# Batch 2's q transposes moved from TensorE to the DMA engines, with the k and q loads of later batches put off

## Chip, cores, metric

One core of a Trainium2 chip. The metric is the device time of the whole program in microseconds (us).

## The reference

Linear attention with an ELU feature map, then two dense layers with a SiLU between, cut to what matters (8 batches, 8 heads, 576 rows, head size 64; the model width is 512, the hidden width 2048):

```python
phi = lambda x: np.where(x > 0, x, np.exp(x) - 1.0) + 1.0
q_p, k_p = phi(q), phi(k)
kv  = einsum('bhsd,bhse->bhde', k_p, v)          # "k product"
num = einsum('bhsd,bhde->bhse', q_p, kv)         # "numerator"
den = einsum('bhsd,bhd->bhs', q_p, k_p.sum(2)) + 1e-6
x   = (num / den) reshaped to 4608 x 512         # "normalisation"
h   = x @ w_in                                   # first phase of a batch
out = (h * sigmoid(beta * h)) @ w_out            # second phase of a batch
```

## The kernel before

TensorE works batch by batch: a first phase (`h_phase`), then a second (`y_phase`). The next batch's attention is threaded between these matmuls by a plan: step number to a list of small jobs. Batch 1's second phase is a special one. It has four output tiles open at once and computes batch 2's attention:

```python
    y_phase_wide(1, {
        1: [F(phi, 2, 1), F(phi, 2, 0)],
        6: [F(kv_mm, 2), F(kv_evac, 2)],
        7: [F(q_trans, 2, 0, 1, wide=True, dve=True)],
        8: [F(q_trans, 2, 2, 3, wide=True, dve=True)],
        9: [F(q_trans, 2, 4, wide=True, dve=True), F(num_mm, 2, 0), F(num_norm, 2, 0)],
        10: [F(num_mm, 2, 1), F(num_norm, 2, 1)],
        11: [F(num_mm, 2, 2), F(num_norm, 2, 2), F(x_trans, 2, 0, wide=True)],
        ...
    def q_trans(b, *ts, wide=False, dve=False):
        ...                                    # 4 transposes on TensorE for each row tile t
        copy(st[b, "qT"][...], tp[...], dve)   # PSUM to SBUF
    def q_trans_dma(b):                        # batches 3 and later do it so already
        nc.sync.dma_start_transpose(out=st[b, "qT"]..., in_=st[b, "p"][:, 0]...)
    def x_trans(b, t, wide=False, dve=False):
        ...                                    # 4 transposes on TensorE into a PSUM bank
        copy(x_dst(b, t), tp[:, :, :n], dve)   # emptied by ScalarE unless dve=True
    def y_phase_wide(b, plan):
        yp = [mm_bank([P, DM]) for _ in range(4)]
        for ff in range(12):
            for t in range(4):
                y_mm(b, yp[t], t, ff)
            run(plan, ff)
        for t in range(4):
            for ff in range(12, FC):
                y_mm(b, yp[t], t, ff)
            y_out(b, t, yp[t], on_act=True)    # output copy on ScalarE
            run(plan, 12 + t)
```

Numerators and wide transposes share two PSUM slots ("att" banks). Ahead of this phase ScalarE makes the exponentials of batch 2, and during it those of batch 3, then loads the SiLU table again (`silu_table`). Loads of k, q and v go through one queue that GpSimd feeds.

## Time and profile before

The time is 296.88 us (median of 3 runs, 296.63 to 297.01); the profiled span is 295.1 us.

| quantity | before |
|---|---|
| TensorE busy | 285.1 us, 97% |
| ScalarE busy | 175.5 us, 59% |
| VectorE busy | 125.2 us, 42% |
| start of batch 1's second phase | 67.15 |
| from there to batch 2's first phase | 18.91 us |
| from there to batch 3's k product | 30.60 us |

The last two rows are my rulers. Both are differences of start times in TensorE's timeline, so the start-up, which shifts by up to 0.9 us from run to run, drops out of them. (Timeline lines are merged: a row stands for a run of like instructions.) In a timeline line the columns are start, duration, engine, source line, operation, tiles and shapes, count, and in brackets the idle time just before with what ended it. Durations of matmuls overlap, so costs are taken from differences of starts.

### The profile page before, as it was taken

The page shows a single profiled execution, that of the slowest core. Times are in us where ns is not written, and L with a number is a line of the kernel's source. Part 1 is how long each engine was busy: PE and PEld are TensorE (multiplying, and loading weights), DVE is VectorE, ACT ScalarE, POOL GpSimd, SP SyncE. Part 2 cuts the span into 40 slices and gives each one's busy share as a digit, 9 for nine tenths or more (in the row PEclk, how much of TensorE's full clock was granted, in tenths as well). Part 3 has the DMA queues.
Part 4 walks back from the last instruction along what each step waited for, and adds up shares of the span by engine and source line. Part 5 has one row for each costly group of instructions (what it writes and reads, how often), then busy time and mean ns, then how long its engine had stood idle before and what let it go on. Part 6 is the DMA issues. An engine that isn't in the chain of part 4 may idle for free.

```text
span 295.1 us, 4791 instructions
## 1 busy us (share of the span) xinstructions
PE 285.1 (97%) x1911; PEld 144.9 (49%) x1932; DVE 125.2 (42%) x264; ACT 175.5 (59%) x234; POOL 52.2 (18%) x72
## 2 busy tenths in 40 slices
PE   8979999999999999999999999999999999999994
PEld 2557445644565544445444544454445444444443
DVE  5675388504772174616461646164715400110012
ACT  2798786889988770778077808790770077018500
POOL 8925475544006000320020000000000000000000
PEclk9999999999999999999999999999999999999998
DMA  7999999999939943698357445024502400120032
GB/s 109 189 205 344 255 273 192 257 193 190 164 142 150 180 93 98 130 177 151 98 128 79 73 116 126 2 72 115 127 0 73 117 36 0 38 94 13 2 71 71
DMA packets 69719, 36.43 MB, mean 123 GB/s; under 512 B 38321, under 2 KB 64193, under 8 KB 69697
## 3 DMA queue, kind: packets, MB, share of 16 engines
q0 software_dynamic: 38912, 20.45, 47.7%
q1 hardware_dynamic: 30624, 15.55, 21.0%
q8 instruction: 15, 0.25, 0.4%
q10 hardware_dynamic: 160, 0.13, 0.2%
q14 instruction: 8, 0.06, 0.0%
HBM read 36.71 MB, written 9.44 MB: 156 GB/s over the span
## 4 chain that ended last, share of the span: by engine, by line
PE 71%; DMA 17%; ACT 4%; POOL 4%; issue 3%; DVE 0%; POOLq 0%; ACTq 0%
PE mm L453 33%; PE mm L505 32%; DMA xqk<-in_q_dram 9%; DMA vraw<-in_v_dram 4%; DMA w_in<-in_moe_w_in_dram 4%; PE att L399 2%; ACT e L229 2%; POOL xqk L131 1%; PE att L344 1%; PE mm L537 1%; ACT L229 1%; POOL vraw L131 1%; ACT g L445 1%; POOL w_in L159 1%; ACT L445 0%
## 5 line engine op out<-in xcount | busy, mean ns | idle before, releaser
L445 ACT ACTIVATE g<-mm,beta_c 128x512 bf16<-128x512 f32 (+2 forms) x156 | 97.3, 633 | 88.1 <-PE mm L453 87.8
L505 PE MATMUL mm<-w_out,g 128*128 128x512 bf16 x541 | 127.2, 379 | 1.2 <-issue 0.3
L453 PE MATMUL mm<-xT,w_in 128*128 128x512 bf16 (+2 forms) x560 | 107.8, 349 | 1.2 <-DMA w_in<-in_moe_w_in_dram 0.8
L453 PEld LDWEIGHTS <-w_in 128*128 128x128 bf16 x656 | 62.0, 98 | 62.0 <-DMA w_in<-in_moe_w_in_dram 1.0
L505 PEld LDWEIGHTS <-g 128*128 128x128 bf16 x560 | 52.7, 98 | 57.3
L515 DVE COPY y_sb<-mm 128x512 f32<-128x512 f32 x27 | 18.7, 692 | 70.4 <-PE mm L505 67.4
L229 ACT ACTIVATE e<-xqk 128x2560 bf16<-128x2560 bf16 x14 | 31.9, 2329 | 0.1
L415 DVE TENSOR_TENSOR xs<-att,rden 128x512 bf16<-128x512 f32 (+1 forms) x40 | 27.6, 689 | 1.6 <-DVE rden L414 0.2
L242 DVE TENSOR_TENSOR qk_p<-r,e 128x2560 bf16<-128x2560 bf16 x14 | 20.9, 1490 | 13.1 <-ACT e L229 12.4
L355 DVE CAST kv_bd<-att 64x130 bf16<-64x130 f32 x28 | 8.2, 292 | 34.5 <-PE att L344 34.1
L72 POOL DMA_DIRECT2D vraw<-in_v_dram x7 | 6.8, 972 | 77.4 <-DVE vaug L370 70.9
L413 DVE TENSOR_SCALAR den<-att 128x8 f32<-128x8 f32 (+1 forms) x40 | 6.5, 162 | 27.0 <-PE att L399 26.8
L399 PEld LDWEIGHTS <-q_pT 128*128 128x128 bf16 (+1 forms) x160 | 11.7, 100 | 10.7 <-DVE xs L415 2.1
L399 PE MATMUL att<-kv_bd,q_pT 128*128 128x130 bf16 (+1 forms) x160 | 15.8, 221 | 1.1 <-DVE kv_bd L370 0.7
L453 PE MATMUL mm<-xT_tail,w_in 128*128 128x512 bf16 x63 | 13.9, 379 | 0.1
L237 DVE TENSOR_SCALAR r<-xqk 128x2560 bf16<-128x2560 bf16 x14 | 11.9, 858 | 3.9 <-DMA xqk<-in_q_dram 2.3
L572 PE MATMUL mm<-g 128*128 128x512 bf16 x34 | 10.4, 468 | 1.2 <-DVE g L143 1.2
L72 POOL DMA_DIRECT2D xqk<-in_k_dram x7 | 8.0, 1150 | 10.2 <-ACT e L229 3.6
L229 ACT ACT_TABLE_LOAD x7 | 9.0, 1283 | 0.1
L414 DVE RECIPROCAL rden<-den 128x8 f32<-128x8 f32 (+1 forms) x40 | 8.1, 201 | 1.4
L72 POOL DMA_DIRECT2D xqk<-in_q_dram x7 | 6.5, 924 | 6.9 <-ACT g L445 2.1
L256 ACT ACTIVATE e<-xqk 128x1280 bf16<-128x1280 bf16 (+1 forms) x4 | 4.4, 1154 | 5.1 <-DMA xqk<-in_k_dram 4.6
(72 smaller groups left out, 142.5 us busy)
## 6 DMA issues: line engine op xcount, KB each, us to landing
out_dram<-y_sb SPq DMA_DIRECT2D x28, 256.0 KB, 2.3
xqk<-in_k_dram POOLq DMA_DIRECT2D x7, 512.0 KB, 10.7
xqk<-in_q_dram POOLq DMA_DIRECT2D x7, 512.0 KB, 11.8
vraw<-in_v_dram POOLq DMA_DIRECT2D x7, 512.0 KB, 11.5
w_in<-in_moe_w_in_dram POOLq DMA_DIRECT2D x4, 512.0 KB, 11.3
g<-in_moe_w_out_dram POOLq DMA_DIRECT2D x4, 512.0 KB, 10.9
out_dram<-y_sb SPq DMA_DIRECT2D x14, 128.0 KB, 5.1
xqk<-in_moe_w_out_dram POOLq DMA_DIRECT2D x2, 512.0 KB, 14.3
```

Source lines behind the costliest of these rows:

```text
L72: eng.dma_start(out=dst[:, :, 0:NJ, :].rearrange("p h j d -> p h (j d)"), in_=src[b, :, 0:MAIN, :].rearrange("h (p j) d -> p h (j d)", j=NJ),)
L229: nc.scalar.activation(st[b, "e", a][:, h0:h1], xqk[b % NX][:, a, h0:h1], ACTF.Exp)
L237: nc.vector.tensor_scalar(st[b, "r", a][:, h0:h1], xqk[b % NX][:, a, h0:h1], 0.0, 1.0, ALU.max, ALU.add)
L242: nc.vector.tensor_tensor(st[b, "p"][:, a].rearrange("p j (h d) -> p h j d", h=H)[:, h0:h1], st[b, "r", a][:, h0:h1], st[b, "e", a][:, h0: ...
L355: nc.vector.tensor_copy(kv_bd[b % 2][i][gs, :, g, :], st[b, "kvp"][gs, 2 * i : 2 * i + 2, :])
L399: nc.tensor.matmul(nps[:n, p // 2, c0 : c0 + 2 * (D + 1)], st[b, "qT"][:, t, p, :n], kv_bd[b % 2][p // 2][:, p % 2], start=True, stop=True ...
L415: nc.vector.tensor_mul(xs[:n], nv[:, :, :, 0:D], rden[:n, :, :, None].to_broadcast([n, 2, 4, D]))
L445: nc.scalar.activation(g_sb[b % 2][:, ff, c0:c1], hp[:, c0:c1], ACTF.Silu, scale=beta_c[:, ff : ff + 1],)
L453: nc.tensor.matmul(hp[:, c0:c1], w_in_sb[ff // 4][:, kc, (ff % 4) * P : (ff % 4 + 1) * P], x[:, t0:t1, kc, :] if b < B else x[:, kc, c0:c1 ...
L505: nc.tensor.matmul(yp, g_sb[b % 2][:, ff, t * P : (t + 1) * P], w_out_sb[ff // 4][:, ff % 4, :], start=(ff == 0), stop=(ff == FC - 1),)
L515: nc.vector.tensor_copy(y_sb, yp)
L572: nc.tensor.matmul(st["warm"], g_sb[0][:, FC - 1, 0:P], g_sb[0][:, FC - 1, :], start=True, stop=True, skip_group_check=True,)
```

## The change

The intent: take 20 transposes off the engine that bounds the kernel. phi(q) is made ahead of phi(k) so that the DMA transpose can start early; batch 5's k and q, which would share the DMA engines with it, are loaded behind batch 5's v, which is held back by a buffer. What is left moves later.

```diff
     def load_next(b):
         if b < B:
+            if b >= 5:
+                load_v(b)
             load_k(b)
             load_q(b)
-            load_v(b)
+            if b < 5:
+                load_v(b)
 ...
-            8: [F(begin, 2), F(relu, 2, 1)],
-            10: [F(relu, 2, 0)],
+            8: [F(begin, 2), F(relu, 2, 0)],
+            10: [F(relu, 2, 1)],
 ...
-    h_last(1, xT[1], [F(exp_, 2, 1), F(exp_, 2, 0)])
+    h_last(1, xT[1], [F(exp_, 2, 0), F(exp_, 2, 1)])
 ...
-        1: [F(phi, 2, 1), F(phi, 2, 0)],
+        1: [F(phi, 2, 0), F(q_trans_dma, 2), F(phi, 2, 1)],
         6: [F(kv_mm, 2), F(kv_evac, 2)],
-        7, 8, 9: q_trans of row tiles 0 to 4;  9 to 13: numerators 0 to 4;  11 to 14: x_trans 0 to 3
+        11: [F(num_mm, 2, 0), F(num_norm, 2, 0)],
+        12: [F(num_mm, 2, 1), F(num_norm, 2, 1), F(x_trans, 2, 0, wide=True)],
+        13: [F(num_mm, 2, 2), F(num_norm, 2, 2), F(x_trans, 2, 1, wide=True)],
+        14: [F(num_mm, 2, 3), F(num_norm, 2, 3)],
 ...                                      # batch 2's first phase
-            plan = {1: [F(x_trans, 2, 4)]}
+            plan = {
+                0: [F(x_trans, 2, 2), F(num_mm, 2, 4), F(num_norm, 2, 4)],
+                1: [F(x_trans, 2, 3)],
+                3: [F(x_trans, 2, 4)],
+            }
```

(The line "7, 8, 9" sums up eight removed lines.)

## The prediction

> **What bounds the kernel now.** I read the busy line first, then the chain of waits, then the timelines of TensorE (PE), ScalarE (ACT) and VectorE (DVE) through the one stretch that the change edits, then the DMA view. The page:
>
> ```profile
> PE 285.1 (97%) x1911; PEld 144.9 (49%) x1932; DVE 125.2 (42%) x264; ACT 175.5 (59%) x234; POOL 52.2 (18%) x72
> PEclk9999999999999999999999999999999999999998
> ```
>
> PE is busy 97% of 295.1 us at the full clock, so a lasting gain must take work or stalls out of PE's stream. The edited stretch is batch 1's second matmul phase: 64 matmuls of 512 columns, with batch 2's attention threaded between. Its first matmul starts at 67.15 and batch 2's first phase at 86.06, 18.91 us later. PE in its second half:
>
> ```profile
> 73.28 0.82 PE L344 MATMUL att<-vaug,qk_p 128*64 128x65 bf16 x40
> 74.27 0.81 PE L505 MATMUL mm<-w_out,g 128*128 128x512 bf16 x3 [0.16 <-issue]
> 74.91 0.61 PE L380 MATMUL att<-identity,qk_p 128*128 128x128 bf16 x8
> 75.36 1.03 PE L505 MATMUL mm<-w_out,g 128*128 128x512 bf16 x4
> ...
> 77.63 0.29 PE L380 MATMUL att<-identity,qk_p 64*128 64x64 bf16 x4
> 77.85 0.41 PE L399 MATMUL att<-kv_bd,q_pT 128*128 128x130 bf16 x4
> 78.09 1.02 PE L505 MATMUL mm<-w_out,g 128*128 128x512 bf16 x4
> ...
> 80.57 0.40 PE L433 MATMUL att<-identity,xs 128*128 128x128 bf16 x4
> 81.02 0.81 PE L505 MATMUL mm<-w_out,g 128*128 128x512 bf16 x3
> 82.12 0.39 PE L399 MATMUL att<-kv_bd,q_pT 128*128 128x130 bf16 x4 [0.29 <-ACT xT L372]
> ```
>
> L380 is the q transposes that go, L399 the numerator, L433 the x transposes, L505 the main matmuls. Durations overlap, so costs come from differences of starts: four main matmuls take 0.86 (75.36 to the next L380 at 76.22), four numerator matmuls 0.24, four x transposes 0.22. Gaps with no work: 80.28 to 80.57 (0.29), 81.66 to 82.12 (0.46; one matmul record of the four seems missing), and 0.10 before the last numerator: 0.85 us lost. ScalarE explains the largest:
>
> ```profile
> 75.51 4.56 ACT L229 ACTIVATE e<-xqk 128x2560 bf16<-128x2560 bf16 x2
> 80.09 1.28 ACT L578 ACT_TABLE_LOAD   x1
> 81.38 0.20 ACT L578 ACTIVATE small<-small 128x1 f32<-128x1 f32 x1
> 81.49 0.58 ACT L372 ACTIVATE xT<-att 128x512 bf16<-128x512 bf16 x1
> 81.97 0.59 ACT L513 ACTIVATE y_sb<-mm 128x512 f32<-128x512 f32 x1
> ```
>
> Batch 3's exponentials and the return to the SiLU table hold ACT until 81.49; only then can it empty the first x transpose's PSUM bank, for which PE stands at 82.12. The chain of waits follows ACT here, not PE.
>
> **What the Trainium skill says.** "VectorE: DVE Perf Modes", section "The three transpose paths", gives 390 ns on TensorE and 1309 ns by DMA for one 128x128 block. Alone, PE is the faster; in a stream the trace has 8 transposes in 0.45 us (74.91 to 75.36), 56 ns each, so the price on PE is far less than 390. "DMA: Bandwidth & Descriptors", section "Queues, rings and completion order", says each DMA engine takes turns between the queues with work, packet by packet; so a transpose beside loads is slowed, not locked out. The trace agrees: 128 KB stores of batch 0, beside saturated loads, landed in 5.3 us (median), those at the end alone in 2.3. "ScalarE: Activation LUTs", section "What ACT_TABLE_LOAD costs", says about 1283 ns for a switch; the page here has 7 of mean 1283.
>
> **The change part by part.**
>
> 1. *Removed from PE:* 5 groups of 4 transposes. Two groups of 8 cost 0.45 each, the tail's 4 cost 0.22 (77.63 to 77.85): 1.12 us of PE's own stream. This is the whole direct gain.
>
> 2. *Removed from DVE:* three copies of q_pT, 0.69 + 0.69 + 0.29 = 1.67 us. DVE is 42% busy; nothing on the path.
>
> 3. *Swapped:* q's exp and phi come before k's. phi(q) takes 68.26 to 69.75, phi(k) 70.49 to 71.98. K's product starts on PE at 73.28, so the swap leaves 1.3 us; no cost.
>
> 4. *Added:* one 640 KB DMA transpose, issued at about 69.8. Those of later batches:
>
> ```profile
> q_pT<-qk_p SPq DMA_TRANSPOSE x5, 4.9
> ```
>
> Alone it would land at 74.7. The loads in flight are the question:
>
> ```profile
> 69.80:75.50 5.70, 5.54 (x69) 3.06 (x69) 2.66 (x5) 5.65 (x7) 1.85 (x3) 1.00 1.59 191
> 75.50:80.00 4.50, 4.50 (x37) 2.46 (x35) 3.24 (x9) 4.49 (x2) 0.00 (x0) 1.00 1.54 183
> 80.00:82.00 2.00, 1.65 (x12) 0.84 (x12) 1.54 (x4) 1.97 (x5) 0.00 (x0) 1.00 0.32 26
> ```
>
> The last two columns are DMA share and GB/s: loads saturate the engines until 80. Batch 4's v (issued 63.34, landing 11.5 us later) fills the time to about 75.5; batch 5's k and q, issued at 68.5 and 71.2, fill 75.5 to 80. The change takes the second part away. So the transpose shares only with v: stretched by 5.3/2.3 for some 6 to 8 us, then alone. At 1/2.3 speed for 6.5 us it does 2.8 of its 4.9; the rest brings it to about 78.4. My estimate is a landing at 77 to 79.
>
> 5. *Moved:* batch 5's k and q are issued behind v(5), which waits for batch 3's vaug copy on DVE. That copy ends at 90.4 now, and some 2 us later once the last normalisation stands before it (part 6); batch 3's k product needs it only near 97. The loads would land near 108 and are first read by the exponentials in batch 3's second phase, near 131. Batches 6 and 7 move back by one v in the same way (landing near 137 and 167, read near 161 and 191). No cost.
>
> 6. *Later plan:* the first numerator now follows step 11, the last numerator and two x transposes move into batch 2's first phase. The work is the same (0.24 + 0.22 + 0.22 = 0.68 us moved).
>
> **Walking PE through the new order.** K's product ends at 74.05 in both. Five steps of 0.86 bring PE to 78.36. Numerator 0 to 78.60; main matmuls to 79.45; numerator 1 to 79.69. X transpose 0 needs DVE's normalisation: in the trace that ends 1.57 us after its numerator starts (77.85 to 79.42), so 79.93, and PE goes on at 79.99 (0.30 lost) to 80.22. Main matmuls to 81.08, numerator 2 to 81.31. X transpose 1 takes the PSUM bank of x transpose 0 (the built program puts both in bank 6), which ACT must empty. ACT is free at 81.49 as before, but its order is now first the output copy, which takes 0.48 of it, then the xT copy of 0.58: done at 82.55, PE goes on at 82.61. That is 1.30 us lost. From there: transpose 0.22, main matmuls 0.86, numerator 3 0.24, main matmuls 0.86: 84.79. Add the 0.68 moved on: 85.47 stands against 86.06. Gain: 0.59 us. Check by sums: 1.12 removed, stalls of 0.30 + 1.30 in place of 0.85, rest rounding.
>
> In batch 2's first phase the same walk, bank by bank, gives no new stall: ACT runs some 0.1 us ahead of each bank that PE wants. After that all is PE-bound (gaps of about 0.2 us a batch at most), so the shift is carried to the end: 296.88 - 0.59 = 296.3.
>
> **The rivals.**
>
> *The full gain.* If ACT's wait were not there, PE would keep 1.12 us and lose only the 0.30: 0.85 + 1.12 - 0.30 = 1.67, giving 295.2. Against it: exp, table load and copies on ACT are untouched by the change, and end at 81.49 whatever PE does. The removed work frees PE to arrive earlier at the same wait. That is why I take half of 1.12.
>
> *The transpose lands late.* It is needed at 78.36 by numerator 0. But PE has the 1.30 us wait ahead of it anyway: a landing up to about 79.5 only shifts idle time from one place to the other. Beyond that each us costs one. If the 2.3 stretch held to the end it would land at 69.8 + 11.3 = 81.1, 1.6 late: 297.9. For it: the engines are saturated to 75.5 and the transpose itself delays v. Against it: the loads of k and q are gone, and a transpose issued at 134.48, as batch 7's loads ended, landed in 2.4, the usual time. I give this one in eight.
>
> *ACT becomes the bound of batch 2's first phase.* Two xT copies (0.48 each) move between its first SiLUs. The margin I found is 0.1 us; a miss costs 0.2 to 0.4 and gives 296.6.
>
> *Later loads come late.* Margins of 24 us say no; were it so, the loss would show from 131 on.
>
> **Range and chances.** Centre 296.3. Repeats spread 0.4 us (296.63 to 297.01). With the late landing and the ACT margin above, and a smaller stall than I walk through below, the range is 295.6 to 297.1. 2% is 5.9 us: the gain cannot exceed the 1.12 plus the 0.85, and the worst landing costs 1 net. So faster 0.01, same 0.98, slower 0.01.
>
> **What would show it right or wrong.** Right: no L380 for batch 2 on PE; the new transpose issued near 69.8 and landing by 79.5; numerator 0 at 78.4; a wait of about 1.3 us before x transpose 1, put down to ACT's xT copy, ending near 82.6; DMA share falling after 76 to 78 instead of 80; batch 2's first phase starting near 84.8 and everything from 101 on about 0.6 earlier. Wrong: numerator 0 waiting on the DMA beyond 79.5; PE passing x transpose 1 before 82 (then the gain nears 1.7); gaps in batch 2's first phase; or any wait for xqk in later batches.

## The result

The changed kernel takes 296.31 us (median of 4 runs, 295.93 to 296.85) against 296.94 (4 runs, 296.63 to 297.04). The ratio is 0.9982, 95% interval 0.9964 to 0.9999. A ratio here is the mean time of one kernel's runs over that of the other's in the same rounds, so it is not quite the ratio of the medians. Executions over 1.5% slower than the fastest of the same kernel are left out of the means.

The two profiled spans are both 295.1 us, though the changed kernel is the faster: its profiled run began the edited phase at 67.61 instead of 67.15, before anything that the change touches. Hence the rulers. The busy line of the page after:

```profile
PE 283.9 (96%) x1891; PEld 143.9 (49%) x1912; DVE 124.0 (42%) x261; ACT 175.1 (59%) x234; POOL 52.7 (18%) x72
```

Twenty matmuls fewer, on an engine still busy 96%. TensorE's timeline through the edited phase of the changed kernel:

```profile
73.75 0.82 PE L344 MATMUL att<-vaug,qk_p 128*64 128x65 bf16 x40
74.73 4.26 PE L505 MATMUL mm<-w_out,g 128*128 128x512 bf16 x19 [0.16 <-issue]
79.33 0.41 PE L399 MATMUL att<-kv_bd,q_pT 128*128 128x130 bf16 x4 [0.34 <-DMA q_pT<-qk_p]
...
82.06 0.40 PE L399 MATMUL att<-kv_bd,q_pT 128*128 128x130 bf16 x4
83.07 0.38 PE L433 MATMUL att<-identity,xs 128*128 128x128 bf16 x4 [0.61 <-ACT xT L372]
...
85.25 0.60 PE L453 MATMUL mm<-xT,w_in 128*128 128x256 bf16 x4
85.69 0.39 PE L433 MATMUL mm<-identity,xs 128*128 128x128 bf16 x4
86.00 0.42 PE L399 MATMUL att<-kv_bd,q_pT 128*64 128x130 bf16 x4
86.36 0.61 PE L453 MATMUL mm<-xT,w_in 128*128 128x256 bf16 x4
86.80 0.39 PE L433 MATMUL mm<-identity,xs 128*128 128x128 bf16 x4
```

The q transposes (L380) are gone. Two waits stand in their place: one for the DMA transpose ahead of numerator 0 (0.34 in the bracket; 0.51 by the starts, 11.72 us into the phase where unhindered runs below have 11.21), and a second one ahead of x transpose 1, put down to ScalarE's copy. (The profile calls that one 0.61; from the starts, 82.06 + 0.24 = 82.30 to 83.07, it is 0.77.) Batch 2's first phase begins at 85.25, 17.64 us into the phase. ScalarE in the same kernel:

```profile
80.55 1.28 ACT L581 ACT_TABLE_LOAD   x1
81.85 0.20 ACT L581 ACTIVATE small<-small 128x1 f32<-128x1 f32 x1
81.95 0.58 ACT L513 ACTIVATE y_sb<-mm 128x512 f32<-128x512 f32 x1
82.43 0.59 ACT L372 ACTIVATE xT<-att 128x512 bf16<-128x512 bf16 x1
```

It comes back with the SiLU table at the same 14.3 us into the phase as before (81.49 - 67.15 and 81.95 - 67.61), makes the output copy first and empties x transpose 0 at 83.02; TensorE goes on at 83.07. The DMA transpose was issued at 70.30. Its line in the view of the tile q_pT, over all six transposes (the longest is batch 2's), and two stretches of the view by windows (last columns: granted clock, DMA share, GB/s; the share is the time of all packets over the span of the 16 engines, and it can pass 1):

```profile
DMA to landing us min/median/max: 4.8/5.3/9.0
```

```profile
69.80:75.50 5.70, 5.54 (x63) 2.86 (x63) 2.76 (x5) 5.65 (x7) 0.00 (x0) 1.00 1.56 169
75.50:80.00 4.50, 4.17 (x23) 1.81 (x21) 0.52 (x4) 4.49 (x3) 0.00 (x0) 1.00 0.46 103
```

It landed at 70.3 + 9.0 = 79.3. The load of batch 4's v fills the first window as before; the second has fallen from a share of 1.54 to 0.46, because batch 5's k and q are no longer there.

### The profile page after: what moved, and what is told of

Its sections match the earlier page's. It is cut to its first block, busy times and chain, and to the rows that moved or that the text cites. A ratio compares the mean times of both kernels' runs of the same rounds, so it can differ in the third digit from the quotient of the medians.

```text
span 295.1 us, 4750 instructions
## 1 busy us (share of the span) xinstructions
PE 283.9 (96%) x1891; PEld 143.9 (49%) x1912; DVE 124.0 (42%) x261; ACT 175.1 (59%) x234; POOL 52.7 (18%) x72
## 4 chain that ended last, share of the span: by engine, by line
PE 76%; DMA 9%; POOL 4%; ACT 4%; issue 4%; DVE 1%; ACTq 0%; POOLq 0%; DVEq 0%
PE mm L453 37%; PE mm L505 33%; DMA xT<-in_moe_w_out_dram 5%; DMA vraw<-in_v_dram 4%; PE att L399 3%; ACT e L229 2%; POOL xqk L131 1%; PE att L344 1%; PE mm L537 1%; POOL w_in L159 1%; ACT L229 1%; POOL vraw L131 1%; ACT g L445 1%; DVE qk_p L242 0%; POOL xqk L111 0%
## 5 line engine op out<-in xcount | busy, mean ns | idle before, releaser
L72 POOL DMA_DIRECT2D xqk<-in_k_dram x7 | 6.9, 984 | 6.3 <-DMA w_in<-in_moe_w_in_dram 2.8
L76 POOL DMA_DIRECT2D xqk<-in_k_dram x7 | 7.4, 1057 | 1.5 <-DMA w_in<-in_moe_w_in_dram 1.3
## 6 DMA issues: line engine op xcount, KB each, us to landing
xqk<-in_q_dram POOLq DMA_DIRECT2D x7, 512.0 KB, 11.3
vraw<-in_v_dram POOLq DMA_DIRECT2D x7, 512.0 KB, 11.3
```

The costliest lines, as they stand in the source:

```text
L72: eng.dma_start(out=dst[:, :, 0:NJ, :].rearrange("p h j d -> p h (j d)"), in_=src[b, :, 0:MAIN, :].rearrange("h (p j) d -> p h (j d)", j=NJ),)
```

## The experiments

All of them in one table, each row from the timeline of that run's profile. "Numerator 0" and "phase" count from the phase's first main matmul; "rest" is from numerator 0 to the end of the phase; "to k product" reaches to batch 3's k product; landing is from the transpose's issue.

| run | start | numerator 0 | rest | phase | to k product | landing | ratio to before (95%) |
|---|---|---|---|---|---|---|---|
| before | 67.15 | 10.70 | 8.21 | 18.91 | 30.60 | | |
| changed | 67.61 | 11.72 | 5.92 | 17.64 | 30.23 | 9.0 | 0.9982 (0.9964 to 0.9999) |
| e5, changed again | 66.89 | 12.14 | 5.50 | 17.64 | 30.23 | 9.4 | 0.9993 (0.9978 to 1.0009) |
| e1, loads not put off | 67.52 | 17.03 | 7.08 | 24.11 | 36.69 | 14.3 | 1.0230 (1.0214 to 1.0246) |
| e7, the same kept busy | 67.31 | 18.32 | 5.15 | 23.47 | 36.05 | 15.6 | 1.0156 (1.0137 to 1.0175) |
| e2, loads put off alone | 66.83 | 10.70 | 8.21 | 18.91 | 30.60 | | 0.9991 (0.9978 to 1.0005) |
| e3, x copy 0 on VectorE | 66.71 | 12.82 | 5.23 | 18.05 | 30.63 | 10.1 | 0.9984 (0.9970 to 0.9997) |
| e4, v(4) later | 67.29 | 11.21 | 6.42 | 17.63 | 30.22 | 5.1 | 0.9991 (0.9977 to 1.0004) |
| e6, v(4) later, both copies | 67.23 | 11.22 | 5.22 | 16.44 | 29.02 | 5.0 | 0.9954 (0.9937 to 0.9971) |
| e9, e6 again | 67.00 | 11.22 | 5.22 | 16.44 | 29.02 | 5.1 | 0.9954 (0.9941 to 0.9966) |
| e8, before with both copies | 67.19 | 10.71 | 8.77 | 19.48 | 31.16 | | 1.0033 (1.0019 to 1.0046) |

### e1: the transpose, but the loads not put off

```diff
-            if b >= 5:
-                load_v(b)
             load_k(b)
             load_q(b)
-            if b < 5:
-                load_v(b)
+            load_v(b)
```

> The changed kernel with the old load order (k, q, v for every batch), so that batch 5's k and q are issued as soon as batch 2's exponentials are done, about 71 to 73. The phase is measured from the first main matmul of batch 1's second phase (67.61 in the profile after, 67.15 before) to the first main matmul of batch 2's first phase: 18.91 us before, 17.64 after. My theory: loads then saturate the DMA engines to about 81, the transpose, which took 9.0 us beside v(4) alone, takes 11 us or more, numerator 0 waits until about 14 us into the phase instead of 11.7, and the part of that beyond the ScalarE wait is lost: phase 18.5 to 19.5 us, time 0.8 to 1.8 us longer than the changed kernel's. Rival (the two loads did not matter, because v(4) alone already stretches the transpose): landing 9 us, phase 17.6, same time as the changed kernel.

Measured: 303.79 us (4 runs), 6.5 us longer in the phase than the changed kernel and 2.3% slower than before. The direction was the theory's, the size was far beyond it: I had expected 0.8 to 1.8 us. The timeline of TensorE and three windows of this run:

```profile
84.55 0.61 PE L399 MATMUL att<-kv_bd,q_pT 128*128 128x130 bf16 x4 [5.65 <-DMA q_pT<-qk_p]
84.96 1.91 PE L505 MATMUL mm<-w_out,g 128*128 128x512 bf16 x4
86.66 0.64 PE L399 MATMUL att<-kv_bd,q_pT 128*128 128x130 bf16 x4
```

```profile
78.00:79.00 1.00, 0.90 (x5) 0.20 (x2) 0.00 (x0) 1.00 (x2) 0.00 (x0) 1.00 1.45 71
82.00:83.00 1.00, 0.00 (x0) 0.00 (x0) 0.00 (x0) 0.00 (x0) 0.00 (x0) 0.67 1.50 201
88.00:89.00 1.00, 1.00 (x4) 0.40 (x3) 0.47 (x1) 0.36 (x1) 0.00 (x0) 0.50 0.65 233
```

Two things are new. First, the transpose took 14.3 us. In the window 78 to 79 the engines are as occupied as ever (share 1.45) but move 71 GB/s; loads alone moved about 190 at such a share. So loads and transpose together can get less done than loads alone, and the stretch is not the fixed 2.3 that I had taken from stores: 14.3 over the 4.9 of a quiet transpose is 2.9. Second, TensorE stood for 5.65 us; the granted clock fell to 0.50 and was still there in the window 88 to 89. Four main matmuls take 86.66 - 84.96 = 1.70 us in place of 0.86.

### e7: the same, with TensorE kept busy

```diff
 # in num_mm, for batch 2's numerator 0 only, on top of e1
+            for _ in range(26):
+                nc.tensor.matmul(nps[:, 0], g_sb[0][:, FC - 1, 0:P], g_sb[0][:, FC - 1, :],
+                                 start=True, stop=True, skip_group_check=True)
```

> The changed kernel with the old load order, where TensorE stood 5.65 us for the transpose and then ran at a granted clock of 0.5 to 0.6 for some 5 us; here 26 idle matmuls of 512 columns (their result is overwritten) fill that wait, 26 x 0.216 = 5.6 us. My theory: the wait for the transpose remains, but the granted clock stays at 1.0 and the phase is 22.2 to 22.6 us instead of 24.11: 5.31 more wait than the changed kernel's 0.34, less the 0.61 of the ScalarE wait, on 17.64. The time is 1.5 to 1.9 us shorter than in the run without them. Rival (the slow matmuls after the wait come from the DMA traffic and not from standing idle): phase 24 again.

```profile
78.53 5.78 PE L399 MATMUL att<-g 128*128 128x512 bf16 x26
85.63 0.40 PE L405 MATMUL att<-kv_bd,q_pT 128*128 128x130 bf16 x4 [1.33 <-DMA q_pT<-qk_p]
85.87 1.02 PE L511 MATMUL mm<-w_out,g 128*128 128x512 bf16 x4
```

```profile
86.00:88.00 2.00, 1.87 (x16) 1.02 (x14) 1.79 (x6) 0.91 (x2) 0.00 (x0) 1.00 1.08 120
```

Measured: the phase is 23.47 us, outside the 22.2 to 22.6 that I had named, because the landing was 1.3 us later still (15.6). What the run was for shows in the column "rest": 5.15 us instead of 7.08, with the clock at 1.00 and main matmuls back at 0.86 (86.73 - 85.87) while loads still ran (share 1.08). So 1.93 us of e1's loss was the clock. The whole loss against the changed kernel adds up: 5.31 later at numerator 0, 0.77 less wait for ScalarE, 1.93 of slow clock, 6.47 together. The medians, 303.79 and 301.47, differ by 2.3 in spite of the later landing, but come from different calls, and the profiled execution of e7 was its slowest (302.37; the fastest took 300.60). "TensorE: Matmul & The Clock Gate" of the Trainium skill, section "HAM oscillation — how this bites in real kernels", gives the rule "no PE-idle gaps >~3.4µs"; e1 agrees: TensorE stopped near 78.9 and the clock fell within the window 82 to 83. That window's mean of 0.67 puts the fall near 82.3 (an estimate), 3.4 us after the stop.

### e2: the loads put off, without the transpose

```diff
 # kernel before, only load_next as in the change
```

> The kernel before with only the new load order (batches 5 to 7: v first, then k and q); q transposes on TensorE as before. My theory: nothing on TensorE waits for these loads, so the phase stays at 18.9 us and the time within 0.15 us of the kernel before. Rival (the gain comes from quieter DMA engines and not from the transposes): it shows the 0.4 to 0.6 us gain by itself.

Measured: both rulers to the hundredth as before, 18.91 and 30.60. The time, 296.58 us against 297.00, leans by 0.3 (by the ratio) but its interval holds 1. The loads are no gain by themselves; they are what the transpose needs in order not to cost 6.5 us.

### e3: x transpose 0 emptied by VectorE

```diff
-        12: [F(num_mm, 2, 1), F(num_norm, 2, 1), F(x_trans, 2, 0, wide=True)],
+        12: [F(num_mm, 2, 1), F(num_norm, 2, 1), F(x_trans, 2, 0, wide=True, dve=True)],
```

> The changed kernel with batch 2's first x transpose emptied by VectorE instead of ScalarE. In the profile after, x transpose 1 waits 0.61 us for ScalarE's copy of x transpose 0 (start 83.07, 15.46 us into the phase). My theory: that wait is what eats half of the gain; with VectorE the copy starts when normalisation 1 ends, 14.4 us into the phase, and lasts about 0.35, so x transpose 1 starts near 14.85: phase 17.0 us instead of 17.64 and the time 0.5 to 0.6 us shorter than the changed kernel's. Rival (the late landing of the transpose, or VectorE's own chain behind it, is the bound): x transpose 1 moves by less than 0.2 us and the time stays.

```profile
79.53 0.40 PE L399 MATMUL att<-kv_bd,q_pT 128*128 128x130 bf16 x4 [1.44 <-DMA q_pT<-qk_p]
...
82.58 0.38 PE L433 MATMUL att<-identity,xs 128*128 128x128 bf16 x4
```

Measured: not what I expected. The ScalarE wait is gone (the line of x transpose 1 has no bracket) and "rest" fell from 5.92 to 5.23, but numerator 0 came 1.10 us later in the phase, so the phase is 18.05. This run began the phase at 66.71, earlier than the others, while the transpose landed at 69.4 + 10.1 = 79.5. Landings on the clock of the span are 79.3 (changed), 79.5 (here) and 79.0 (e5), while the phase begins anywhere from 66.71 to 67.61: the landing goes with the end of v(4)'s load (which landed at about 75.6, 76.2 and 75.6 in the same three runs), and an early start only waits longer. In this run the DMA wait had taken the whole place of ScalarE's. That is no clean test of the copy alone: with numerator 0 at 11.72, as in the changed kernel's profile, this "rest" would give a phase of 11.72 + 5.23 = 16.95 (an estimate), 0.69 shorter. The ratios, 0.9984 here against 0.9982 and 0.9993, show no gain.

### e5: the changed kernel once more

> The changed kernel once more, unaltered, for a second trace and more rounds. The landing of the transpose seems tied to the end of v(4)'s load and not to its issue (79.3 after an issue at 70.3 in the profile after, 79.5 after an issue at 69.4 in the run with the VectorE copy). My theory: it lands again at 79.0 to 80.0 from the span's start, and the phase is 17.6 to 18.1 us long, longer the earlier it starts; time 0.998 of the kernel before. Rival (a landing of 9 us whatever the loads do): 17.6 always.

```profile
79.03 0.40 PE L399 MATMUL att<-kv_bd,q_pT 128*128 128x130 bf16 x4 [0.75 <-DMA q_pT<-qk_p]
...
82.36 0.38 PE L433 MATMUL att<-identity,xs 128*128 128x128 bf16 x4 [0.21 <-ACT xT L372]
```

Measured: landing at 69.6 + 9.4 = 79.0 as the theory says, and yet the phase is 17.64 to the hundredth: it was not longer for the earlier start, as I had thought, and the rival's number came out without its reason. The DMA wait grew by 0.42 (numerator 0) and the wait for ScalarE shrank by 0.42 ("rest"). One wait takes over from the other. The ratio here, 0.9993, and the first one, 0.9982, have overlapping intervals; the ruler's 0.37 us, 0.12% of 297, lies between them.

### e4: batch 4's v loaded later

```diff
+            if b == 5:
+                load_v(4)          # behind v(5), about 94 instead of 63
             load_k(b)
             load_q(b)
-            if b < 5:
+            if b < 4:
                 load_v(b)
```

> The changed kernel with batch 4's v loaded after batch 5's v (about 95) instead of at 63 to 75, so that the transpose has the DMA engines nearly to itself. My theory: it lands 5 to 6.5 us after issue instead of 9.0, numerator 0 runs without a wait at about 11.2 us into the phase instead of 11.72, but x transpose 1 still waits for ScalarE until 15.4 to 15.5, so the phase stays 17.6 and the time within 0.15 us of the changed kernel. Rival (the landing is the bound): phase 17.1 and 0.5 us shorter.

```profile
78.50 0.40 PE L399 MATMUL att<-kv_bd,q_pT 128*128 128x130 bf16 x4
...
82.75 0.38 PE L433 MATMUL att<-identity,xs 128*128 128x128 bf16 x4 [1.12 <-ACT xT L372]
```

Measured: as expected. The transpose lands in 5.1 us, numerator 0 no longer waits, and the ScalarE wait takes up all of it: phase 17.63. Nearly four microseconds off the landing bought nothing.

### e6 and e9: v(4) later and both x copies on VectorE

```diff
 # on top of e4
-        12: [F(num_mm, 2, 1), F(num_norm, 2, 1), F(x_trans, 2, 0, wide=True)],
-        13: [F(num_mm, 2, 2), F(num_norm, 2, 2), F(x_trans, 2, 1, wide=True)],
+        12: [F(num_mm, 2, 1), F(num_norm, 2, 1), F(x_trans, 2, 0, wide=True, dve=True)],
+        13: [F(num_mm, 2, 2), F(x_trans, 2, 1, wide=True, dve=True), F(num_norm, 2, 2)],
```

> v(4) loaded later as in the run of that name, and both x transposes of the phase (0 and 1) emptied by VectorE, the second ahead of normalisation 2. Both things that hold the phase are then gone. My theory: numerator 0 at 11.2 us into the phase, x transpose 1 at 14.25 instead of 15.46, and the phase 16.4 us instead of 17.63, so the time 1.2 us below the changed kernel and 1.6 below the one before (ratio about 0.9945). Rival (another wait of ScalarE, its output copies or the first SiLUs of batch 2, takes over at once): phase above 17.2, or the gain lost again before batch 3's k product (30.2 us after the start of the phase in the changed kernel; I expect 29.0).

> The kernel with v(4) later and both x copies on VectorE once more, on the same chip as the run beside it, to see whether the phase of 16.44 us and the ratio of 0.9954 repeat: phase 16.4 to 16.5, ratio 0.994 to 0.997.

```profile
78.45 0.39 PE L399 MATMUL att<-kv_bd,q_pT 128*128 128x130 bf16 x4
...
81.49 0.38 PE L433 MATMUL att<-identity,xs 128*128 128x128 bf16 x4
...
83.67 0.60 PE L453 MATMUL mm<-xT,w_in 128*128 128x256 bf16 x4
```

Measured (the lines are of e6): phase 16.44 and k product at 29.02 in both runs, medians 295.21 and 295.56 us, ratio 0.9954 twice. No line has a bracket; x transpose 1 stands 14.26 us into the phase. This version beats both kernels. With the changed kernel, e3 and e4 it makes a square of two waits: ending only ScalarE's (e3, in its one trace) or only the DMA's (e4) gave no shorter phase, ending both gives 1.20 us.

### e8: the same copies without the change

```diff
 # kernel before
-        11: [F(num_mm, 2, 2), F(num_norm, 2, 2), F(x_trans, 2, 0, wide=True)],
-        12: [F(num_mm, 2, 3), F(num_norm, 2, 3), F(x_trans, 2, 1, wide=True)],
+        11: [F(num_mm, 2, 2), F(x_trans, 2, 0, wide=True, dve=True), F(num_norm, 2, 2)],
+        12: [F(num_mm, 2, 3), F(x_trans, 2, 1, wide=True, dve=True), F(num_norm, 2, 3)],
```

> The kernel before (q transposes on TensorE) with x transposes 0 and 1 emptied by VectorE, each ahead of the normalisation it stood behind: the cure that took 1.2 us off the changed kernel, applied without the change. My theory: with the q transposes still on TensorE the ScalarE wait before numerator 3 was only 0.46 us, and VectorE's own chain stands right behind it (normalisation 2 would end near 82.5 where x transpose 1 wants its bank at 81.9), so the phase falls from 18.91 to between 18.5 and 18.9 us and the time by at most 0.4. Rival (the 1.2 us came from the copies alone and owe nothing to the DMA transpose): the phase falls to 17.7.

```profile
82.56 0.38 PE L433 MATMUL att<-identity,xs 128*128 128x128 bf16 x4 [0.46 <-DVE xs L415]
...
84.50 0.38 PE L433 MATMUL att<-identity,xs 128*128 128x128 bf16 x4 [0.34 <-DVE xs L415]
```

Measured: slower, 297.54 us, phase 19.48. Both theory and rival missed. The copies put the normalisations off, and TensorE now waits for VectorE twice: x transpose 1 goes on at 82.56 when normalisation 2 has ended (82.51), x transpose 2 at 84.50 when normalisation 3 has (84.44). Their own inputs were ready before, so they must have waited for the bank that the numerator of that normalisation held; this follows from the times and was not tested. The gain of e6 is not to be had by these copies in the old plan. Whether another placing would do it there was not tried.

## Why the prediction was right

- *1.12 us of transposes removed.* The 20 matmuls went; numerator 0 in the unhindered runs (e4, e6) stands at 11.2 into the phase, as walked (78.36 - 67.15 = 11.21).
- *The loads must be put off.* The reason given, sharing the DMA engines, is right. What they would cost was never worked out: the worst landing that I named, 11.3 us after issue, was for the changed kernel; with the loads left in place e1 had 14.3 and e7 15.6, and I did not reckon with the clock.
- *Landing at 77 to 79.* It was 79.3, 79.0 and (e3) 79.5, up to half a microsecond late. The step that failed is the stretch "At 1/2.3 speed for 6.5 us", and with it "slowed, not locked out". In the DMA view of short windows the transpose's queue (q1) moved no packet in the changed kernel before 73.2, 2.9 us after the issue, while the loads kept their 185 to 195 GB/s; in e4, and alone before the change (issue 119.6), the first packet came after 1.2 us. From 73.2 it caught up as v(4) ran out: 0.44 of its 0.66 MB by 76.3, or 67% where the forecast was 2.8 of 4.9, 57%. So the landing came near the forecast by another course than the one forecast. The statement that a late landing up to about 79.5 only moves idle time held: e5 shows 0.42 us changing sides, e4 shows the whole wait on ScalarE's side. With a start at 67.61 or 66.89 the limit moves along, to about 80.0 or 79.2.
- *The ScalarE wait eats half.* Right, and it is the centre of the prediction. Predicted 1.30 us; 0.77 in the changed kernel because the landing had taken the rest; 81.22 + 0.24 to 82.75, so 1.29, in e4 where the landing is out of the way. The phase came out at 17.64 as walked (84.79 - 67.15). With this wait and the DMA's gone (e6), the gain is 30.60 - 29.02 = 1.58, near the 1.67 of the rival "The full gain".
- *0.68 us moved into batch 2's first phase.* This term was too small. From the end of the phase to batch 3's k product it is 11.69 us before and 12.58 to 12.59 in every run with the new plan, whatever else was changed: 0.90. The numerator of the last, 64-row tile starts 0.09 late and takes 0.36 (86.00 to 86.36), not 0.24. I had counted its 0.10 before as a stall that would go, but it is the tile's own price and moved with it. So the gain that the trace shows is 18.91 - 17.64 - 0.90 = 0.37 us, not 0.59. The prediction's own check by sums had warned of it: 1.12 + 0.85 - 0.30 - 1.30 is 0.37, and the 0.22 that was put down to rounding is as much as the moved work was short of (0.90 - 0.68). That it meets the trace to the hundredth is chance in part: the sum leaves out 0.10 that went with the 64-row q transposes (76.67 to 77.63 is 0.96, not 0.86) and counts the 0.10 that stayed. Repeats are too scattered to tell these apart: the medians say 0.63 and 0.32, so that the first one, 296.31, meets the centre of 296.3 is luck.
- *ScalarE as the bound of batch 2's first phase, and late loads in later batches:* not seen. The first would have varied that 12.58 between runs in which ScalarE had two copies fewer (e6) or not; it did not. TensorE waits for no load after 67.

What stays open: why loads and a transpose together move so little (71 GB/s in the worst window). The DMA view says where the time goes: in e1's window 78 to 79 the transpose's queue moved 201 packets at a share of 118.5%, beside 38 packets of loads; in the changed kernel's 76 to 77, with no load left, 1131 at 127.7%. Each packet of the transpose took about five times as long, and nothing here says why. That the landing goes with the end of v(4)'s load is shown by e4 and the three landings; the mechanism inside the DMA engines is not.

## What to carry to other kernels

Work taken off the bounding engine is worth only what the next wait on its path leaves of it. Walk the new order bank by bank up to the first wait that does not move: here it was ScalarE coming back from a table load, and it left a third of 1.12 us until a second engine took the copies over. When two waits stand side by side, each can hide the other, and curing one may show nothing until the other is cured too. A DMA transpose should be given a quiet stretch: beside loads it took two to three times as long here, and in e1 the wait was long enough to take TensorE's clock with it.

## What the Trainium skill lacked or had wrong

- "DMA: Bandwidth & Descriptors", section "Queues, rings and completion order", has the turns between queues but not what sharing costs a transpose. A transpose of 640 KB (655,360 bytes) landed in 4.8 to 5.1 us alone or nearly so, 9.0 to 10.1 beside one load of 576 KB (v), 14.3 and 15.6 beside three such loads (v, k, q); throughput of all together fell to 71 GB/s in one window where loads alone moved about 190. Beside loads at full rate (changed kernel) its first packet came 2.9 us after the issue, alone and in e4 after 1.2.
- "Advanced Engine Details and Errata", section "X-Bar Transpose (TRN2)", expects 350 to 400 GB/s. Here 640 KB in 4.8 us from issue to landing, the fastest, is 137 GB/s with the fixed latency; while packets moved it was 223 GB/s (e4, 72 to 74) and 290 in the best microsecond (changed kernel, 76 to 77).
- "VectorE: DVE Perf Modes", section "The three transpose paths", gives 390 ns for a TensorE transpose without saying that this is one by itself (the page "TensorE: Matmul & The Clock Gate" does say so, and has about 275 ns within one kernel). In a stream 8 took 0.45 us here, 56 ns each.
- "TensorE: Matmul & The Clock Gate", section "Back-to-back issue gap", gives 131 ns a matmul at 512 columns and 81 ns at 128 as sustained in a real kernel. Here four of 512 took 0.86 us at the full clock, 215 ns each, and transposes of 128 columns 56 ns, with weight loads between them in both. That is what the same section's formula for the isolated gap gives (216 and 56 ns), which it says is too high at 512 and too low at 128 for a stream.
